# Row sums and exponential sums of an attention block moved between GpSimd, VectorE and TensorE

## The chip, the cores and the metric

The kernel runs on one core of a Trainium2 chip. A core has four engines that compute, each with an instruction queue of its own: TensorE (PE in the profile; PEld is its weight load), VectorE (DVE), ScalarE (ACT) and GpSimd (POOL). SyncE (SP) issues the DMAs. An engine takes its instructions in order; between engines the order is kept by semaphores. The metric is the device time of one execution in microseconds, median over runs.

## The reference

Two blocks follow each other. The first is attention with normalised queries and keys, for 8 batches of 12 heads, 448 positions, 64 elements a head:

```
q_n = q / sqrt(mean(q*q) + 1e-6) * g_q          # the same for k
scores = q_n @ k_n^T / 8
attn   = exp(scores - max); attn /= sum(attn)
x      = attn @ v                                # (8,12,448,64) -> (3584, 768)
```

The second takes the 3584 rows of x through `h = x @ w_in` (768 to 1024), `solu = h * softmax(h)`, a layer norm with gain, and `@ w_out` (1024 to 768). The change touches the first block only, in two places: the mean of squares under the square root, and the sum of the exponentials.

## The kernel before

Only `fast_path` runs on these inputs. Heads are taken four at a time: a quad m, of which there are 24 (0 to 23), is two pairs, a = 2m and b = 2m + 1, and a pair n is two heads. After the quads come the first product of the second block (line 989) and the last one (line 1203), each built of fewer, larger products of sums of blocks.

The order of all instructions is written out by hand, in the loop over m from line 1383 (`tc.manual_schedule()`), and each engine works in the order in which its instructions are emitted there. `unit(f)` emits a piece and then whatever was put off with `later`. The loop works on several quads at once. In the body of quad m:

- TensorE computes the scores of quad m, keys along partitions (`scores`, line 818): three tiles of 128 keys for each pair, `E0`, `E1`, `E2`, and one tile, `scores_last` (line 831), that holds the last 64 keys of both pairs. ScalarE takes the exponential of each as it comes (line 808; tiles of 128 x 896, two heads by 448 queries).
- Then `values_last` and `values` (lines 860 and 871) multiply the exponentials by v, and `sums` (line 890) adds the exponentials over the keys by products with a constant of ones, 32 columns wide, so that four of them fill the columns of the array. To spare TensorE some of these, VectorE has added `E0` and `E1` beforehand (`add`, line 845, tile `es`). In quads 0 to 21 `sums` runs over five tiles (the last keys, `E2` of each pair, `es` of each pair), each as four products; in the last two quads VectorE adds `E2` too (`add_more`, line 850) and `sums` runs over three.
- `inverse` transposes the sums and takes the reciprocal on VectorE (lines 901 and 902), and GpSimd copies parts of it across partitions (line 909, four small copies). In the next quad `divide` (lines 916 and 917) applies it and `store_x` writes x to memory.
- Beside it, quad m prepares what later quads need. `norms_next` completes 1/sqrt(mean of squares) for quad m + 1: two ScalarE instructions (lines 700 and 701) and four small ones on VectorE (lines 707 to 710, result `ny`), after which GpSimd scales q and k of the two pairs (`normalise`, line 719), VectorE transposes them (`qk_transpose`, line 729) and ScalarE applies the gains (line 733). For quad m + 2, ScalarE squares (line 662), VectorE sums 32 elements at a time (`row_sums`, line 670, tile `part`), and GpSimd joins the two halves of a head, which lie in neighbouring groups of 32 partitions: `fold_sums` copies the four groups across (line 680) and adds (line 681), which gives `ss`.
- Some quads convert a piece of w_in from 64-bit input: ScalarE (lines 535 and 536) in quads 4 to 10, 12, 14, 16, 18, 20, and VectorE's `join` (lines 541 and 542) one quad later each. `combine_in` (line 563, on GpSimd) forms differences of w_in blocks, in quads 9, 11, 13, 14, 15, 17, 19, 21 (one each) and 22, 23 (two each).

VectorE's order within quad m, from quad 5 on, is: reciprocal of quad m - 1 (901, 902), the four of `ny`, `divide` of quad m - 1, two transposes (729), `add(a)`, `row_sums` of pair a + 4, `row_sums` of pair b + 4, `add(b)`, and the join where there is one. GpSimd's is: copies of quad m - 1 (909), two `normalise`, `combine_in` where there is one, `fold_sums`.

PSUM tiles with tag "t" have three buffers of two banks each, shared by the score tiles and the sums tile; the pairs' outputs `o` have two buffers.

Of the kernel before, what the change touches and what calls it, by code (L numbers as in the profile page):

```python
# [9 lines left out]
FP32 = mybir.dt.float32  # L10
# [4 lines left out]
OP = AluOpType  # L15
# [351 lines left out]
def fast_path(  # L367
# [24 lines left out]
    nc = tc.nc  # L392
    B, H, S, D = q.shape
    DM, DFF = moe_w_in.shape
    P = 128
    NJ = S // P
    NB = S // 32
    NP = H // 2
    NQ = B * NP // 2
# [12 lines left out]
    consts = ctx.enter_context(tc.tile_pool(name="consts", bufs=1))  # L412
# [7 lines left out]
    work = first.enter_context(tc.tile_pool(name="work", bufs=2))  # L420
    ps_t = banks_in.enter_context(tc.tile_pool(name="ps_t", bufs=3, space=bass.MemoryType.PSUM))
    w_out = conv = sums_in = None

    ident = consts.tile([P, P], FP32, name="ident")
    ones = consts.tile([P, 3, 32], FP32, name="ones")

# [47 lines left out]
    def norm_gain():  # L474
        pg = ps_t.tile([P, KF], FP32, tag="t", name="pg")
        nc.tensor.transpose(pg, grow, ident[0:KF, 0:KF])
        nc.scalar.copy(gcol[:, 0:KF], pg)
# [81 lines left out]
    def combine(b, i):  # L559

        b11, b21, b22, t1, t3, t2, t4 = b
        o, p, q = [(t3, b22, t1), (t1, t1, b11), (t2, b22, t1), (t4, b21, t2)][i]
        nc.gpsimd.tensor_tensor(o, p, q, OP.subtract)  # L563

    def combine_in(x):
        c, i = divmod(x, 4)
        combine([w_in[k][:, c] for k in range(7)], i)
# [50 lines left out]
    st = {}  # L618
    quads = {}
    norms = {}  # L620
# [38 lines left out]
    def squares(n):  # L659
        d = st[n]  # L660
        d["sq"] = work.tile([P, 2 * NB, 32], FP32, tag="sq", name="sq", bufs=2)
        nc.scalar.activation(d["sq"].rearrange("p (s b) d -> p s (b d)", s=2), d["qk"], AF.Square)
# [3 lines left out]
    def row_sums(n):  # L666
        m, i = divmod(n, 2)
        if i == 0:
            norms[m] = {"part": small.tile([P, 2, 2 * NB], FP32, tag="part", name="part", bufs=2)}
        nc.vector.tensor_reduce(norms[m]["part"][:, i], st[n]["sq"], AX, OP.add)  # L670
# [3 lines left out]
    def fold_sums(m, e=nc.gpsimd):  # L674
        d = norms[m]
        part = d["part"].rearrange("p i b -> p (i b)")
        ss = d["ss"] = small.tile([P, 4 * NB], FP32, tag="ss", name="ss", bufs=2)
        for g in range(4):
            o = g ^ 1
            e.tensor_copy(ss[g * 32 : g * 32 + 32], part[o * 32 : o * 32 + 32])  # L680
        e.tensor_tensor(ss, ss, part, OP.add)
# [21 lines left out]
    def rsqrt_step(d):  # L703
# [5 lines left out]
        nc.vector.tensor_tensor(x, x, y, OP.mult)  # L709
        nc.vector.scalar_tensor_tensor(y, x, 1.5, y, OP.add, OP.mult)  # L710

    def normalise(n, e=nc.gpsimd):
        d = st[n]
        if ("one", n) in norms:
            y = norms["one", n]["y"]
        else:
            y = norms[n // 2]["y"][:, n % 2 * 2 * NB : (n % 2 + 1) * 2 * NB]
        d["qkn"] = work.tile([P, 2 * NB, 32], FP32, tag="qkn", name="qkn", bufs=2)
        e.tensor_tensor(  # L719
            d["qkn"].rearrange("p (s b) d -> p s b d", s=2),  # L720
            d["qk"].rearrange("p s (b d) -> p s b d", d=32),
            y.rearrange("p (s b) -> p s b ()", s=2).to_broadcast([P, 2, NB, 32]),
            OP.mult,
        )

    def qk_transpose(n):
        d = st[n]
        d["qkT"] = work.tile([P, 2, S], FP32, tag="qkT", name="qkT", bufs=3)
        nc.vector.transpose(d["qkT"].rearrange("p s t -> p (s t)"), d["qkn"].rearrange("p b d -> p (b d)"))  # L729
# [76 lines left out]
    def exponentials(d, kc, s):  # L806
        d["E", kc] = big_tile("E")[:, 0 : 2 * S].rearrange("p (h t) -> p h t", h=2)
        nc.scalar.activation(d["E", kc], s[:, :, 0:S], AF.Exp)  # L808

    def scores(n, kc):  # L810
        d = st[n]
        s = ps_t.tile([P, 2, 512], FP32, tag="t", name="s")

        for c in range(0, P, D):
            for h in range(2):
                hh = slice(h * D, (h + 1) * D)
                keys = slice(NJ * c + kc, NJ * (c + D - 1) + kc + 1, NJ)
                nc.tensor.matmul(  # L818
                    s[c : c + D, h, 0:S], d["qkT"][hh, 1, keys], d["qkT"][hh, 0, :],
                    start=True, stop=True,  # L820
                )
        exponentials(d, kc, s)
# [16 lines left out]
    def on_vector(m):  # L839
        return m >= NQ - 2  # L840

    def add(n):
        d = st[n]
        d["es"] = work.tile([P, 2, S], FP32, tag="es", name="es")
        nc.vector.tensor_tensor(d["es"], d["E", 0], d["E", 1], OP.add)  # L845

    def add_more(n):
        d = st[n]
        if on_vector(n // 2):
            nc.vector.tensor_tensor(d["es"], d["es"], d["E", 2], OP.add)  # L850
# [25 lines left out]
    def sums(m):  # L876


        d = quads[m]
        sm = d["sm"] = ps_t.tile([P, S // 2], FP32, tag="t", name="sm")  # L880
        terms = [(2, d["E", NJ])]
        for key in ("es",) if on_vector(m) else (2, "es"):
            for i in range(2):
                n = st[2 * m + i]
                terms.append((i, n["E", 2] if key == 2 else n["es"]))
        for x, (w, e) in enumerate(terms):
            for h in range(2):
                for t in range(2):
                    g = 32 * (2 * h + t)
                    nc.tensor.matmul(  # L890
                        sm[g : g + 32, :], ones[:, w], e[:, h, t * S // 2 : (t + 1) * S // 2],
                        start=(x == 0), stop=(x == len(terms) - 1),
                    )

    def inverse(m):


        d = quads[m]
        r = work.tile([P, NB // 2, 32], FP32, tag="r", name="r", bufs=1)
        rc = d["rc"] = small.tile([P, 2, 2, NB // 2], FP32, tag="rc", name="rc")  # L900
        nc.vector.transpose(r.rearrange("p b i -> p (b i)"), d["sm"])
        nc.vector.reciprocal(
            rc, r[:, :, 0:32:16].rearrange("p b i -> p i () b").to_broadcast([P, 2, 2, NB // 2])
        )
        for h in range(2):
            for t in range(2):
                a = 64 * h + 32 * t
                o = 64 * h + 32 * (1 - t)
                nc.gpsimd.tensor_copy(rc[o : o + 32, :, t], rc[a : a + 32, :, t])
# [405 lines left out]
    def unit(f, steps=4):  # L1315
        nonlocal now
        f()
        now += steps
        due = [x for x in todo if x[0] <= now]
        todo[:] = [x for x in todo if x[0] > now]  # L1320
        for _, g in sorted(due, key=lambda x: x[0]):
            g()
# [5 lines left out]
    joins_at = {9: (0,), 11: (1,), 13: (2,), 14: (3,), 15: (4,), 17: (5,), 19: (6,), 21: (7,), 22: (8, 9), 23: (10, 11)}  # L1328
# [34 lines left out]
    with tc.manual_schedule():  # L1363
# [19 lines left out]
        for m in range(NQ):  # L1383
            a, b = 2 * m, 2 * m + 1
# [9 lines left out]
            if m == 0:  # L1394
# [5 lines left out]
                for s in range(2):  # L1400
                    transpose_rows(1, s)
                    take_rows(1, s)
                squares(2)
                add(a)
                row_sums(2)
                fold_one(2)
# [10 lines left out]
                rsqrt_seed(norms["one", 3])  # L1417
                rsqrt_step(norms["one", 3])
                normalise(3)
                qk_transpose(2)  # L1420
                gain(2)
                add(b)
                unit(outputs)
                squares(4)
                qk_transpose(3)
                gain(3)
                unit(lambda: values(b))
                squares(5)
                unit(lambda: sums(m))
                inverse(m)  # L1430
                row_sums(4)
# [5 lines left out]
            def norms_next():  # L1437
                rsqrt_seed(norms[m + 1])
                rsqrt_step(norms[m + 1])
                normalise(a + 2)  # L1440
                normalise(b + 2)

            if early:
                norms_next()
            for x in joins_at.get(m, ()):
                combine_in(x)
            if next1:
                load_v(m + 1)
            if m == 1:
# [21 lines left out]
            unit(lambda: scores_last(m))  # L1471
            if m == 3:
                norm_gain()
            if m < 2:
                add(a)
            unit(lambda: scores(b, 0))
# [5 lines left out]
            unit(lambda: scores(b, 1))  # L1482
            if early or 1 < m < 4:
                qk_transpose(b + 2)
            if m > 1:
                add(a)
            unit(lambda: scores(b, 2))
            if m == 1:
                qk_transpose(a + 2)
            scarce = m < 5  # L1490
# [13 lines left out]
            if scarce and m > 1:  # L1504
                squares(b + 4)
                add(b)
            if next2:
                row_sums(b + 4)
                fold_sums(m + 2)
            if not scarce:  # L1510
                add(b)
            add_more(a)
            add_more(b)
            unit(outputs)
# [82 lines left out]
        for n in range(NS):  # L1597
            base = period * n
            for i, name in enumerate(ORDER):
# [4 lines left out]
                x = HALVES[name][0]  # L1604
# [118 lines left out]
```

## Time and profile before

| | us |
|---|---|
| median of 3 runs (lowest, highest) | 816.29 (816.02, 816.68) |
| the profiled execution | 815.47 |
| its span, first to last instruction | 813.7 |
| TensorE busy in the span | 797.9 |
| VectorE, ScalarE, GpSimd busy | 617.0, 473.9, 469.0 |
| one quad, from quad 5 to 21 | 12.90 |

The sums below are made against the profiled execution: span 813.7 us and 1.8 us outside it, 815.47 us, which is 0.8 us under the median. The attention block ends 325.5 us after the start, the first product of the second block at about 560 us. TensorE's rows count two instructions for each fp32 product. Starts and durations are in us unless marked ns; the text after an arrow in brackets names what ended the idle time before an instruction.

### The profile page before, as it was taken

The page shows a single profiled execution, that of the slowest core. Times are in us where ns is not written, and L with a number is a line of the kernel's source. Part 1 is how long each engine was busy: PE and PEld are TensorE (multiplying, and loading weights), DVE is VectorE, ACT ScalarE, POOL GpSimd, SP SyncE. Part 2 cuts the span into 40 slices and gives each one's busy share as a digit, 9 for nine tenths or more (in the row PEclk, how much of TensorE's full clock was granted, in tenths as well). Part 3 has the DMA queues.
Part 4 walks back from the last instruction along what each step waited for, and adds up shares of the span by engine and source line. Part 5 has one row for each costly group of instructions (what it writes and reads, how often), then busy time and mean ns, then how long its engine had stood idle before and what let it go on. Part 6 is the DMA issues. An engine that isn't in the chain of part 4 may idle for free.

```text
span 813.7 us, 14586 instructions
## 1 busy us (share of the span) xinstructions
PE 797.9 (98%) x5030; PEld 468.4 (58%) x5030; DVE 617.0 (76%) x1217; ACT 473.9 (58%) x785; POOL 469.0 (58%) x635
## 2 busy tenths in 40 slices
PE   8999999999999999999999999999989999999997
PEld 4334444444444443444444444444679999999996
DVE  6877889888887977478878756777796876866945
ACT  6677878777786865365767545444515454464420
POOL 1353555656555566233356467767497867777761
PEclk9999999999999999999999999999999999999999
DMA  9868798887878644245755344552548457365412
GB/s 165 175 143 157 165 184 185 188 178 159 163 162 180 132 94 123 81 131 142 184 142 146 91 113 122 147 137 64 171 122 279 129 197 245 122 239 181 150 60 83
DMA packets 269600, 122.71 MB, mean 151 GB/s; under 512 B 187596, under 2 KB 254668, under 8 KB 269516
## 3 DMA queue, kind: packets, MB, share of 16 engines
q1 hardware_dynamic: 254332, 111.78, 55.1%
q10 hardware_dynamic: 15184, 9.90, 4.5%
q8 instruction: 42, 0.69, 0.4%
q14 instruction: 42, 0.34, 0.1%
HBM read 84.94 MB, written 36.70 MB: 149 GB/s over the span
## 4 chain that ended last, share of the span: by engine, by line
PE 88%; DVE 5%; POOL 2%; DMA 2%; ACT 2%; issue 1%; SPq 0%; DVEq 0%; POOLq 0%; ACTq 0%
PE A L1203 14%; PE A L989 13%; PE o L871 13%; PE s L818 12%; PE B L989 8%; PE B L1203 7%; PE sm L890 5%; PE C L989 4%; PE D L989 4%; PE C L1203 3%; PE o L860 2%; PE s L831 2%; DMA xg<-xd 1%; ACT E L808 1%; DVE bs L1072 1%
## 5 line engine op out<-in xcount | busy, mean ns | idle before, releaser
L808 ACT ACTIVATE E<-s 128x896 f32<-128x896 f32 x168 | 139.1, 937 | 20.3 <-PE s L818 20.0
L818 PE MATMUL s<-qkT 64*64 64x448 f32 x1152 | 120.5, 545 | 1.4 <-ACT E L808 0.7
L871 PE MATMUL o<-E,v 128*64 128x448 f32 x576 | 113.5, 543 | 0.0
L680 POOL COPY ss<-part 32x56 f32<-32x56 f32 x88 | 42.1, 478 | 91.5 <-DVE part L670 88.8
L719 POOL TENSOR_TENSOR qkn<-qk,ny 128x896 f32<-128x896 f32 x46 | 77.1, 1697 | 21.2 <-DMA qk<-in_k_dram 12.0
L1078 POOL TENSOR_TENSOR he<-he,mhalf 128x1 f32<-128x1 f32 x28 | 27.6, 986 | 105.6 <-DVE he L1077 105.1
L1203 PE MATMUL B<-w_out,sums 128*128 128x192 f32 x392 | 80.0, 327 | 3.3 <-DVE P L1265 2.1
L818 PEld LDWEIGHTS s<-qkT 64*64 64x64 f32 x1152 | 48.1, 163 | 59.6 <-ACT E L808 29.2
L1203 PE MATMUL A<-w_out,sums 128*128 128x192 f32 x392 | 80.0, 327 | 1.2 <-POOL sums L1183 0.8
L871 PEld LDWEIGHTS o<-E,v 128*64 128x64 f32 x576 | 39.2, 137 | 72.7 <-issue 67.3
L989 PE MATMUL B<-w_in,xsum 128*128 128x512 f32 x168 | 76.7, 592 | 0.7 <-POOL he L1078 0.7
L989 PE MATMUL A<-w_in,xg 128*128 128x512 f32 x168 | 74.6, 593 | 0.0
L1060 ACT ACTIVATE u<-h,hmax 128x1024 f32<-128x1024 f32 x28 | 32.2, 1148 | 63.4 <-DVE hmax L1054 63.3
L1203 PEld LDWEIGHTS B<-w_out,sums 128*128 128x128 f32 x392 | 66.1, 190 | 4.0 <-DVE P L1265 2.4
L1203 PEld LDWEIGHTS A<-w_out,sums 128*128 128x128 f32 x392 | 66.1, 190 | 2.1 <-POOL sums L1183 1.3
L989 PEld LDWEIGHTS B<-w_in,xsum 128*128 128x128 f32 x168 | 31.8, 190 | 41.2 <-issue 38.3
L989 PEld LDWEIGHTS A<-w_in,xg 128*128 128x128 f32 x168 | 31.8, 190 | 40.1 <-issue 39.6
L845 DVE TENSOR_TENSOR es<-E 128x896 f32<-128x896 f32 x48 | 53.4, 1114 | 1.3 <-ACT E L808 1.3
L670 DVE TENSOR_REDUCE part<-sq 128x28 f32<-128x896 f32 x46 | 48.1, 1078 | 2.4
L729 DVE STREAM_TRANSPOSE qkT<-qkn 128x896 f32<-128x896 f32 x46 | 48.5, 1088 | 1.8 <-POOL qkn L719 1.8
L1203 PE MATMUL A<-w_out,s 128*128 128x192 f32 x224 | 45.5, 326 | 0.0
L563 POOL TENSOR_TENSOR w_out<-w_out 128x384 f32<-128x384 f32 x44 | 44.5, 1017 | 1.3
(151 smaller groups left out, 1622.4 us busy)
## 6 DMA issues: line engine op xcount, KB each, us to landing
ur<-ud SPq DMA_DIRECT2D x60, 256.0 KB, 4.5
ud<-ub SPq DMA_DIRECT2D x112, 128.0 KB, 2.3
xd<-xo SPq DMA_DIRECT2D x48, 224.0 KB, 3.1
qk<-in_q_dram SPq DMA_DIRECT2D x92, 112.0 KB, 3.1
qk<-in_k_dram SPq DMA_DIRECT2D x92, 112.0 KB, 3.0
v<-in_v_dram SPq DMA_DIRECT2D x24, 384.0 KB, 4.4
out_dram<-P SPq DMA_DIRECT2D x19, 384.0 KB, 3.7
raw<-in_moe_w_in_dram SPq DMA_DIRECT2D x12, 512.0 KB, 4.7
```

The lines of the kernel that those rows point to most:

```text
L563: nc.gpsimd.tensor_tensor(o, p, q, OP.subtract)
L670: nc.vector.tensor_reduce(norms[m]["part"][:, i], st[n]["sq"], AX, OP.add)
L680: e.tensor_copy(ss[g * 32 : g * 32 + 32], part[o * 32 : o * 32 + 32])
L719: e.tensor_tensor(d["qkn"].rearrange("p (s b) d -> p s b d", s=2), d["qk"].rearrange("p s (b d) -> p s b d", d=32), y.rearrange("p (s b) - ...
L729: nc.vector.transpose(d["qkT"].rearrange("p s t -> p (s t)"), d["qkn"].rearrange("p b d -> p (b d)"))
L808: nc.scalar.activation(d["E", kc], s[:, :, 0:S], AF.Exp)
L818: nc.tensor.matmul(s[c : c + D, h, 0:S], d["qkT"][hh, 1, keys], d["qkT"][hh, 0, :], start=True, stop=True,)
L845: nc.vector.tensor_tensor(d["es"], d["E", 0], d["E", 1], OP.add)
L871: nc.tensor.matmul(d["o"][h * D : (h + 1) * D, :], quads[n // 2]["v"][:, n % 2 + 2 * h, kc], d["E", kc][:, h], start=False, stop=(kc == NJ ...
L890: nc.tensor.matmul(sm[g : g + 32, :], ones[:, w], e[:, h, t * S // 2 : (t + 1) * S // 2], start=(x == 0), stop=(x == len(terms) - 1),)
L989: nc.tensor.matmul(k[bank], a[:, c], w_in[i][:, c], start=begin and c == 0, stop=c == HD - 1, skip_group_check=not begin,)
L1203: nc.tensor.matmul(k[bank], a[:, c].rearrange("p a i -> p (a i)"), w_out[:, area, i, c], start=begin and c == 0, stop=c == KC - 1, skip_gr ...
```

## The change

In quads 5 to 21 (`settled`):

1. `add_late` puts `E1 + E2` of each pair on GpSimd, and VectorE's `add` then adds `E0` to that. `sums` therefore runs over three tiles instead of five in all quads from 5 on.
2. `fold_sums` is gone. In its place TensorE multiplies `part` by a 128 x 128 constant, `halves`, at the end of `sums`. The result `ss` lies in the second bank of the PSUM buffer whose first bank holds the sums, so this buffer is held until line 707 has read `ss` in the next quad.
3. VectorE's `add(b)` comes before `row_sums` of pair b + 4 and no longer after it; `combine_in` moves on GpSimd from before the scores to after both new additions.

`fill_halves` makes the constant once, on GpSimd, in quad 4.

```
+    def settled(m):
+        return 4 < m < NQ - 2
+    def add_late(n):
+        d = st[n]
+        d["es"] = work.tile([P, 2, S], FP32, tag="es", name="es")
+        nc.gpsimd.tensor_tensor(d["es"], d["E", 1], d["E", 2], OP.add)
     def add(n):
         d = st[n]
+        if settled(n // 2):
+            nc.vector.tensor_tensor(d["es"], d["E", 0], d["es"], OP.add)
+            return
...
-        sm = d["sm"] = ps_t.tile([P, S // 2], FP32, tag="t", name="sm")
+        two = ps_t.tile([P, 2, 512], FP32, tag="t", name="sm")
+        sm = d["sm"] = two[:, 0, 0 : S // 2]
         terms = [(2, d["E", NJ])]
-        for key in ("es",) if on_vector(m) else (2, "es"):
+        for key in ("es",) if m > 4 else (2, "es"):
...
+        if settled(m):
+            d = norms[m + 2]
+            d["ss"] = two[:, 1, 0 : 4 * NB]
+            nc.tensor.matmul(
+                d["ss"], halves, d["part"].rearrange("p i b -> p (i b)"), start=True, stop=True
+            )
...
-            for x in joins_at.get(m, ()):
-                combine_in(x)
+            if not settled(m):
+                for x in joins_at.get(m, ()):
+                    combine_in(x)
...
             unit(lambda: scores(b, 1))
             if early or 1 < m < 4:
                 qk_transpose(b + 2)
+            if settled(m):
+                add_late(a)
             if m > 1:
                 add(a)
             unit(lambda: scores(b, 2))
+            if settled(m):
+                add_late(b)
...
+            if settled(m):
+                add(b)
             if next2:
                 row_sums(b + 4)
-                fold_sums(m + 2)
-            if not scarce:
+                if not settled(m):
+                    fold_sums(m + 2)
+            if m >= NQ - 2:
                 add(b)
+            if settled(m):
+                for x in joins_at.get(m, ()):
+                    combine_in(x)
```

More of the change, by code (lines that the diff above doesn't have):

```diff
@@ L422, in fast_path @@
     w_out = conv = sums_in = None
+    halves = consts.tile([P, P], FP32, name="halves")
     ident = consts.tile([P, P], FP32, name="ident")
@@ L710, in rsqrt_step, with fill_halves @@
         nc.vector.scalar_tensor_tensor(y, x, 1.5, y, OP.add, OP.mult)
+    def fill_halves():
+        x = ident.rearrange("p (h x t) -> p h x t", h=2, x=2)
+        nc.gpsimd.tensor_tensor(
+            halves.rearrange("p (h x t) -> p h x t", h=2, x=2),
+            x[:, :, 0:1].to_broadcast([P, 2, 2, 32]), x[:, :, 1:2].to_broadcast([P, 2, 2, 32]), OP.add,
+        )
     def normalise(n, e=nc.gpsimd):
@@ L893, in sums @@
                     )
+        if settled(m):
[3 more added lines that the diff above has]
+                d["ss"], halves, d["part"].rearrange("p i b -> p (i b)"), start=True, stop=True
+            )
     def inverse(m):
@@ L1473, in fast_path @@
                 norm_gain()
+            if m == 4:
+                fill_halves()
             if m < 2:
```

## The prediction

> **What bounds the kernel now.** I read the engines' totals and the chain that ended last, then the chain in order of time within one quad, then each engine's timeline over the same quad. From the page:
>
> ```profile
> PE 797.9 (98%) x5030; PEld 468.4 (58%) x5030; DVE 617.0 (76%) x1217; ACT 473.9 (58%) x785; POOL 469.0 (58%) x635
> ...
> PE 88%; DVE 5%; POOL 2%; DMA 2%; ACT 2%; issue 1%; SPq 0%; DVEq 0%; POOLq 0%; ACTq 0%
> ```
>
> TensorE is the bound. The chain in order of time (start, duration) shows quad 14, from 197.16:
>
> ```profile
> 197.16 2.45 PE s L818 x24
> 199.61 0.75 PE s L831 x8
> 200.36 2.25 PE s L818 x24
> 202.61 0.75 PE o L860 x8
> 203.37 4.66 PE o L871 x24
> 208.03 2.03 PE sm L890 x40
> ```
>
> These touch one another and add up to 12.9: a quad is 12.90 because TensorE's work is 12.90, and its last 2.03 are the 40 instructions of the sums. The other engines have to come round once in that time; how nearly they fail to is in the timelines of VectorE and GpSimd:
>
> ```profile
> 194.91 0.72 DVE L541 SCALAR_TENSOR_TENSOR tmp<-raw,tmp 128x512 uint32<-128x512 uint32 x1
> 195.66 0.69 DVE L542 SCALAR_TENSOR_TENSOR w_in<-raw,tmp 128x512 uint32<-128x512 uint32 x1
> 197.22 0.42 DVE L901 STREAM_TRANSPOSE r<-sm 128x224 f32<-128x224 f32 x1 [0.87 <-PE sm L890]
> ...
> 198.68 0.22 DVE L710 SCALAR_TENSOR_TENSOR ny<-nx,ny 128x56 f32<-128x56 f32 x1
> ...
> 203.63 1.05 DVE L845 TENSOR_TENSOR es<-E 128x896 f32<-128x896 f32 x1
> 204.81 2.08 DVE L670 TENSOR_REDUCE part<-sq 128x28 f32<-128x896 f32 x2
> 206.80 1.08 DVE L845 TENSOR_TENSOR es<-E 128x896 f32<-128x896 f32 x1
> ```
>
> ```profile
> 199.10 3.36 POOL L719 TENSOR_TENSOR qkn<-qk,ny 128x896 f32<-128x896 f32 x2
> 202.41 1.28 POOL L563 TENSOR_TENSOR w_in<-w_in,w_in 128x512 f32<-128x512 f32 x1
> 207.02 1.75 POOL L680 COPY ss<-part 32x56 f32<-32x56 f32 x4 [3.33 <-DVE part L670]
> 208.85 0.30 POOL L681 TENSOR_TENSOR ss<-ss,part 128x56 f32<-128x56 f32 x1
> ```
>
> VectorE finishes the join of a quad only 0.87 before it has to read the sums. GpSimd has holes, but its two normalise end at 202.46, 5.3 into the quad, and all that is queued behind them starts after that.
>
> **The change part by part.**
>
> *TensorE, less.* Two of five tiles leave the sums: 16 of 40 instructions at 2.03 / 40 = 0.051, so 0.81 a quad. Quad 22 already has that shape.
>
> *TensorE, more.* The product with `halves` is two instructions, 128 x 128 weights and 112 columns. Nearest rows: 8 transposes of 112 x 112 at the start take 1.22, 0.15 each, and 392 instructions of 128 x 192 on line 1203 take 80.0, 0.20 each. So 0.3 to 0.4; I take 0.3. TensorE alone would need 12.90 - 0.81 + 0.30 = 12.39 a quad, 17 x 0.51 = 8.7 us less in all. That is what the change can give.
>
> *GpSimd, less.* Copies and add, 1.75 + 0.30 up to 2.58 + 0.30. They were behind the loop that follows, so removing them yields nothing on the path.
>
> *GpSimd, more.* Two additions of 128 x 896 with two full operands. Undisturbed additions of that kind took 0.725 for 256 columns (minimum 0.724, line 1181), 1.00 for 384 (median of line 563 on w_out) and 1.28 for 512 (median on w_in): 0.00216 us a column and 0.17 fixed, so 2.10 for 896. The lowest bound is `normalise`, also 128 x 896 but with one operand repeated along 32 elements: 1.70. I take 2.10, since shape and operands are those of the three rows; 1.70 and 2.20 stay as ends.
>
> By the Trainium skill's page "GPSIMD Engine Reference", section "Elementwise — side-by-side cycle accounting", a tensor_tensor add of 2048 columns takes 4497 ns, scaled an estimate of 1.97 for ours, and its section "Engine selection" advises VectorE for such an add; at 1.97 the sum below would be 34 x 0.13 = 4.4 lower. No run here shows that row, and the 2.10 of the rows is kept.
>
> *Who has the port.* VectorE's `add` and GpSimd's additions exclude each other, as two places show. At 207.02 the first copy of line 680 meets `add(b)`, started at 206.80, and the four take 1.75 instead of 1.02 as at 79.05. And where VectorE asks just after GpSimd:
>
> ```profile
> 599.79 0.73 POOL L1182 TENSOR_TENSOR sums<-sums,s 128x256 f32<-128x256 f32 x1
> ```
>
> ```profile
> 599.84 1.23 DVE L1164 TENSOR_TENSOR s<-ur 128x512 f32<-128x512 f32 x1
> ```
>
> GpSimd has its undisturbed 0.73, and VectorE, 0.05 later, 1.23 instead of 0.72. Now `add(a)` waits for `add_late(a)`. Released by GpSimd, VectorE starts 0.03 after its end (199.05 after 199.01, lines 916 and 909), while GpSimd's next instruction starts 0.04 before the end of the last, if its inputs are there (two normalise: 3.36 for 2 x 1.70). E2 of pair b is there: ScalarE's seven exponentials end 6.8 into the quad. So `add_late(b)` gets the port first and `add(a)` waits for both, 4.20 after the second normalise. Had VectorE got it, its 1.05 would lie between the two additions, and `add(b)` would come 1.05 sooner. That is the other end.
>
> *VectorE.* Behind the waiting `add(a)` are queued the two row sums, `add(b)`, the join, and line 901 of this quad, which all move back. `add(b)` before the second row sum: 1.05 sooner for TensorE's sums, 1.05 later for `part`, for which the `halves` product now waits, and behind it all scores of the next quad and their exponentials.
>
> *The loop.* From one `ny` (end of line 710) to the next, all in sequence:
>
> - normalise both pairs: 202.46 - 198.90 = 3.56
> - two additions on GpSimd: 4.20
> - add, row sum, add, row sum on VectorE: 1.05 + 1.04 + 1.05 + 1.04 = 4.18
> - with a join: 1.44 for it (194.91 to 196.35), then lines 901 to 710: 198.90 - 197.22 = 1.68. Sum 15.06, with hand-offs 15.1.
> - without a join: the product 0.3 and its hand-off 0.1, lines 700 and 701 0.62 (197.13 to 197.75), lines 708 to 710 0.75, hand-offs 0.1: 1.87. Sum 13.8.
>
> Before, no such loop existed: the adds needed nothing from GpSimd, and the fold came after them with room. Now it outlasts TensorE's 12.39 in every quad, so TensorE waits, for `es` of pair b, then for `part`. Twelve quads have a join (5 to 11, 13, 15, 17, 19, 21), five have none: 12 x 15.1 + 5 x 13.8 = 250.2, against 17 x 12.90 = 219.3: +30.9.
>
> *combine_in, moved.* It has no reader before line 989, so the move itself costs nothing. But it now follows the additions: `add(a)`, which already waits, goes first, then 1.28 of combine_in runs beside 1.04 of row sum and holds `add(b)` for 0.24: eight quads, +1.9. Between nothing and 1.28 each.
>
> *PSUM buffer.* It is wanted by the third score tile, 1.65 into the quad; line 707 reads `ss` at 0.8 now, and some 1.8 in a quad after a join. TensorE has slack there by then. Nothing; 0.2 a quad at most.
>
> *DMA queue and the rest.* No DMA is moved in SP's order; store_x and the loads wait for divide and stretch with the quads. `fill_halves`, one 128 x 128 addition in a GpSimd hole of quad 4: under 0.5, hidden by the 4.6 it idles there. After quad 21 the lateness of `ny` reaches the end by divide, the store and the reload of x for the second block, which in the chain already sets the start of quad 23. Everything later is shifted.
>
> Sum: 30.9 + 1.9 = +32.8 on 815.47: 848.3; on the median, 0.8 more, **849 us**.
>
> **The rivals.**
>
> 1. *VectorE takes the port between the two additions.* Then 17 x 1.05 = 17.9 less, so 831. For it: at 594 to 600 a VectorE instruction that is already waiting gets in between two of GpSimd. Against it: here it isn't yet waiting. 0.13.
> 2. *A cheaper addition.* At 1.70 the loops are 14.3 and 13.0: 34 x 0.40 = 13.6 less, 835. For it: line 719, the same size. Against: the three rows with two full operands. 0.13.
> 3. *Faster: the loop closes in time, and TensorE's saving is all that is left.* One mechanism, the price of GpSimd's addition. With p for it, 12 x (10.9 + 2p) + 5 x (9.6 + 2p) = 219.3 at p = 1.19: below that there is no loss, and at 0.75 the joined loop fits 12.39 and 808 is reached. For it: GpSimd idles 44% of these quads (busy 122.6 of 219.3), and TensorE is 98% busy. Against: no 128 x 896 row of GpSimd is under 1.69. 0.07.
> 4. *More than I count*: combine_in holding `add(b)` fully, or TensorE's pauses dearer: 8 x 1.04 more, 858 and beyond. 0.07.
>
> **How the numbers follow.** My case 0.58, rivals 0.13, 0.13, 0.07, 0.07, and 0.02 for no change. The time is that of my case. Its own range is 841 to 853 (2.0 to 2.2 an addition, combine_in 0 to 0.5). The range of 8 in 10 takes in rivals 1 and 2 with their mid-values and leaves out 3 and most of 4: 826 to 857. A change under 0.2% (1.6 us) can't be told from none. Faster 0.08, same 0.02, slower 0.90.
>
> **What would show it.** Right: GpSimd's additions at 2.1 each, back to back; `add(a)` recorded with some 3 us where its own time is 1.05; quads of 15 and 13.8 us, alternating from 12 on; TensorE idle before `sm`, put down to `es`, and before the scores or the product, put down to `part`; DVE and POOL with large shares of the chain between 81 and 300 us. Wrong: quads of 12.4, no wait of TensorE for line 845; additions under 1.7; or `add(a)` at 1.05 between two additions of GpSimd (rival 1). What happens after 325 us should only be shifted.

## The result

The changed kernel takes 842.79 us (median; 842.55 to 844.07) against 816.15 for the kernel before in the same comparison: a ratio of 1.0331, 95% interval 1.0313 to 1.0349. It is 26.6 us slower. The forecast was 849, with a range from 826 to 857.

The profiled execution's span went from 813.7 to 841.0 us, 27.3 more. TensorE's starts of the first scores of each quad divide it: quads 5 to 21 take 244.9 instead of 219.3 (+25.6), quads 22 and 23 take 25.9 instead of 25.2 (+0.7), and all that follows 489.2 instead of 488.2 (+1.0). So the loss lies in the quads that were changed.

From the page of the changed kernel: the busy times, the chain's shares by engine, and three of the costly groups (busy time, mean ns of one, then idle time ahead of them and what ended it). Line numbers have moved, and differ a little from run to run: 856 is GpSimd's new addition, 861 VectorE's add behind it, 917 the product with `halves`, 927 the transposition of the sums (901 before), 701 the first ScalarE instruction of `ny`, 671 the row sums.

```profile
PE 803.5 (96%) x4792; PEld 462.2 (55%) x4792; DVE 649.1 (77%) x1217; ACT 472.1 (56%) x785; POOL 506.1 (60%) x585
...
PE 62%; DVE 21%; POOL 11%; ACT 2%; DMA 2%; issue 1%; SPq 0%; DVEq 0%; POOLq 0%; ACTq 0%
...
L861 DVE TENSOR_TENSOR es<-E,es 128x896 f32<-128x896 f32 x34 | 67.8, 1993 | 15.3 <-POOL es L856 15.3
...
L856 POOL TENSOR_TENSOR es<-E 128x896 f32<-128x896 f32 x34 | 71.5, 2126 | 0.4 <-ACT E L816 0.4
...
L701 ACT ACTIVATE ny<-sm,eps 128x56 f32<-128x56 f32 x17 | 5.2, 308 | 76.2 <-DVE r L927 76.2
```

From the page of the kernel before, VectorE's add:

```profile
L845 DVE TENSOR_TENSOR es<-E 128x896 f32<-128x896 f32 x48 | 53.4, 1114 | 1.3 <-ACT E L808 1.3
```

TensorE carried 88% of the chain and now carries 62%. VectorE and GpSimd carry 32%, where it was 7%. VectorE's add has a mean of 1993 ns where the same shape took 1114; the mean is of two kinds, as the rows below show, about 2.98 us for `add(a)` and 1.1 for `add(b)`. One turn of the loop, quad 13, is in the chain in order of time (start, duration):

```profile
199.32 3.35 POOL qkn L727 x2
202.67 2.08 POOL es L856
204.75 0.02 issue
204.77 2.98 DVE es L861
207.75 1.00 DVE part L671
208.74 1.09 DVE es L861
209.83 1.00 DVE part L671
210.83 0.61 DVE tmp L542
211.44 0.02 issue
211.46 0.69 DVE w_in L543
212.15 0.34 DVE r L927
212.49 0.02 issue
212.51 0.33 DVE rc L928
212.84 0.01 issue
212.85 0.23 DVE nx L708
...
214.03 3.35 POOL qkn L727 x2
```

TensorE does not appear at all. From `normalise` to the next `normalise` everything is GpSimd's and VectorE's, 14.71 long. (In a quad without a join, TensorE's product is in it, with 0.44.) What TensorE does in the meantime is in its timeline (line 910 is the sums):

```profile
208.11 0.58 PE L910 MATMUL sm<-E,ones 128*32 128x224 f32 x8
208.51 0.56 PE L910 MATMUL sm<-es,ones 128*32 128x224 f32 x8
209.88 0.58 PE L910 MATMUL sm<-es,ones 128*32 128x224 f32 x8 [0.81 <-DVE es L861]
210.88 0.43 PE L917 MATMUL sm<-part,halves 128*128 128x56 f32 x2 [0.41 <-DVE part L671]
```

It waits for `es` of the second pair, then for `part`, the two waits that were forecast.

### The profile page after: what moved, and what is told of

The parts are those of the page before. It is cut to its first block, busy times and chain, and to the rows that moved or that the text cites. A ratio compares the mean times of both kernels' runs of the same rounds, so it can differ in the third digit from the quotient of the medians.

```text
span 841.0 us, 14056 instructions
## 1 busy us (share of the span) xinstructions
PE 803.5 (96%) x4792; PEld 462.2 (55%) x4792; DVE 649.1 (77%) x1217; ACT 472.1 (56%) x785; POOL 506.1 (60%) x585
## 4 chain that ended last, share of the span: by engine, by line
PE 62%; DVE 21%; POOL 11%; ACT 2%; DMA 2%; issue 1%; SPq 0%; DVEq 0%; POOLq 0%; ACTq 0%
PE A L1229 14%; PE A L1015 12%; PE B L1015 8%; DVE es L861 8%; PE B L1229 7%; POOL qkn L727 6%; PE C L1015 4%; DVE part L671 4%; PE D L1015 4%; POOL es L856 4%; PE C L1229 3%; PE o L890 3%; PE s L826 3%; PE sm L910 1%; DVE w_in L543 1%
## 5 line engine op out<-in xcount | busy, mean ns | idle before, releaser
L826 PE MATMUL s<-qkT 64*64 64x448 f32 x1152 | 127.2, 561 | 3.6 <-DVE nx L708 2.1
L826 PEld LDWEIGHTS s<-qkT 64*64 64x64 f32 x1152 | 45.8, 165 | 65.1 <-ACT E L816 33.4
L935 POOL COPY rc<-rc 32x14 f32<-32x14 f32 x96 | 19.8, 206 | 100.1 <-DVE rc L928 86.5
L861 DVE TENSOR_TENSOR es<-E,es 128x896 f32<-128x896 f32 x34 | 67.8, 1993 | 15.3 <-POOL es L856 15.3
L856 POOL TENSOR_TENSOR es<-E 128x896 f32<-128x896 f32 x34 | 71.5, 2126 | 0.4 <-ACT E L816 0.4
L701 ACT ACTIVATE ny<-sm,eps 128x56 f32<-128x56 f32 x17 | 5.2, 308 | 76.2 <-DVE r L927 76.2
```

Of the source, the lines that this page charges most:

```text
L826: nc.tensor.matmul(s[c : c + D, h, 0:S], d["qkT"][hh, 1, keys], d["qkT"][hh, 0, :], start=True, stop=True,)
L856: nc.gpsimd.tensor_tensor(d["es"], d["E", 1], d["E", 2], OP.add)
L861: nc.vector.tensor_tensor(d["es"], d["E", 0], d["es"], OP.add)
```

## The experiments

The theory: the loss is a loop, from `ny` over two normalise and two additions on GpSimd to VectorE's adds, row sums and join, and back to `ny`. It is longer than TensorE's work of a quad. Its rivals: the product with the constant, with `ss` in PSUM, is what costs; or VectorE and GpSimd are too full for any addition on GpSimd; or it does not matter who gets the port they share (by the rows in the prediction, a two-input add of VectorE and an addition of GpSimd exclude each other; "the port" stands for what they exclude each other from). Lengths of a quad below are from TensorE's first score to the next quad's first score, read from each run's timeline.

### The product alone

VectorE and TensorE add as before the change, and VectorE's order is the old one; the product is kept, and with it the new place of `combine_in`. Part of the edit:

```
...
-        for key in ("es",) if m > 4 else (2, "es"):
+        for key in ("es",) if on_vector(m) else (2, "es"):
...
-            if settled(m):
-                add_late(a)
...
-            if settled(m):
-                add_late(b)
...
-            if settled(m):
-                add(b)
...
```

> Only the product with the constant replaces GpSimd's copies in quads 5 to 21; the exponentials are added as before the change (VectorE E0 + E1, TensorE takes E2), and add(b) is again behind the row sums. Loop theory (the loss is the chain from ny over both normalise and both GpSimd additions to VectorE's adds and back to ny): without the additions the chain is short, TensorE is the bound again and pays only for the product, 0.36 a quad in the changed kernel's trace, 17 x 0.36 = 6.1: 822, quads of 13.26, no wait of TensorE for part. Rival, the product theory (the loss is ss in PSUM: TensorE waits for part and line 701 for line 927): quads of 14 and more, above 835.

Measured: 822.65 us (822.27 to 824.43), ratio 1.0087 (1.0071 to 1.0104). Every quad from 5 to 21 takes 13.25 or 13.26. The chain of this run:

```profile
211.13 2.03 PE sm L907 x40
213.16 0.36 PE sm L914 x2
213.52 2.45 PE s L826 x24
```

TensorE goes from the sums to the product to the scores with no pause. The product costs its own 0.36 and nothing else, and the new place of `combine_in` costs nothing by itself. As the cause of the loss the product falls.

### The additions alone

GpSimd keeps the fold of four copies and an add; no product:

```
-        if settled(m):
-            d = norms[m + 2]
-            d["ss"] = two[:, 1, 0 : 4 * NB]
-            nc.tensor.matmul(
-                d["ss"], halves, d["part"].rearrange("p i b -> p (i b)"), start=True, stop=True
-            )
...
-                if not settled(m):
-                    fold_sums(m + 2)
+                fold_sums(m + 2)
```

> Only GpSimd's additions; the fold stays with GpSimd, behind them, as four copies and an add. Loop theory: the loop now has the fold in it. From the changed kernel's rows 3.49 + 5.08 + 1.00 + 1.09 + 1.00 = 11.66 up to the second row sum, then 1.4 fold (2.3 beside a join), 0.66 and 0.75 to ny: 14.5 and 15.4 a quad, and combine_in before the next normalise some 0.9 in eight quads: 854 to 861, say 858, slower than the changed kernel. Product theory: the waits for part go and TensorE saves 0.81 a quad: 802 to 805.

Measured: 858.10 us (857.56 to 859.03), ratio 1.0519 (1.0501 to 1.0537). Quads behind one with a join take 15.3, without one 14.5, and 16.0 behind one with both a join and a combine_in (15.5 behind quad 14, which has a combine_in and no join). TensorE has less work here than in the changed kernel, and the time is the longest of all. In this order of instructions the product thus earned its 0.36: it took GpSimd's fold out of the loop. The two halves of the change do not add up (+6.5 and +42.0 alone, +26.6 together): with the additions in place, the product removes a piece of the loop.

### VectorE's row sums before both adds

```
-            if m > 1:
+            if m > 1 and not settled(m):
                 add(a)
...
-            if settled(m):
-                add(b)
             if next2:
                 row_sums(b + 4)
...
+            if settled(m):
+                add(a)
+                add(b)
```

> As the changed kernel, but VectorE takes both row sums before both adds, so that they fill the time in which it waited for GpSimd. Loop theory: the loop loses both row sums: 3.49 + 5.08 + 1.00 + join 1.30 + 1.75 = 12.6 with a join, and without one TensorE's own 12.45. In the eight quads with a combine_in, that one holds the port between the two adds, 1.2 each. Sum over 17 quads 223.5 against 219.3: 820; 811 if VectorE's second add goes ahead of combine_in. Rival, full engines (the additions and the shared port cost this much in whatever order): 835 to 843, quads of 14 and more.

Measured: 822.65 us (822.09 to 823.16), ratio 1.0079 (1.0063 to 1.0096), 20 us less than the changed kernel by order alone. Row sums wait for nothing of GpSimd and have one input, so they run while GpSimd adds: two of them take 2.08 from 180.85 on, beside two additions of GpSimd that take 4.18 from 178.56 on. Quads without a combine_in take 12.87, those with one 13.65 to 13.95. That GpSimd and VectorE are too full in whatever order is excluded. The second effect, combine_in, shows in the timeline of VectorE, once without and once with:

```profile
182.84 2.08 DVE L861 TENSOR_TENSOR es<-E,es 128x896 f32<-128x896 f32 x2
...
195.57 3.01 DVE L861 TENSOR_TENSOR es<-E,es 128x896 f32<-128x896 f32 x2
```

Two adds take 2.08 alone, and 3.01 when a combine_in takes the port between them (GpSimd's row: 1.28 from 195.35 on). What the new place of `add(b)` in the changed kernel does by itself was not tried.

### Who gets the port, with a wait

A copy of a column of `es` stands between GpSimd's two additions and makes the second wait for VectorE's `add(a)`:

```
             if settled(m):
+                turn = small.tile([P, 1], FP32, tag="turn", name="turn", bufs=2)
+                nc.gpsimd.tensor_copy(turn, st[a]["es"][:, 0, 0:1])
                 add_late(b)
```

> As the changed kernel, but a copy of one column of es of pair a stands between GpSimd's two additions, so that the second can only start when VectorE's add(a) is done: VectorE gets the port in between. Loop theory: add(a) takes 1.0 instead of 2.98, the second addition ends about 1.25 later, add(b) starts 0.5 to 0.6 sooner than in the changed kernel: 17 x 0.55 = 9.4 less, 833. If who goes first did not matter: 843 or some us above, for the copy.

Measured: 842.37 us (841.91 to 843.23), ratio 1.0321 (1.0303 to 1.0338): no gain over the changed kernel, and a miss of 9. By the number alone the port would not matter. The timeline of VectorE says otherwise:

```profile
203.51 1.09 DVE L861 TENSOR_TENSOR es<-E,es 128x896 f32<-128x896 f32 x1 [0.84 <-POOL es L856]
204.52 1.08 DVE L671 TENSOR_REDUCE part<-sq 128x28 f32<-128x896 f32 x1
206.93 2.14 DVE L861 TENSOR_TENSOR es<-E,es 128x896 f32<-128x896 f32 x1 [1.33 <-POOL es L856]
```

`add(a)` fell from 2.98 to 1.09, as expected. But `add(b)`, which now waits for the second addition directly, meets the same race again: combine_in is next in GpSimd's queue, and `add(b)` takes 2.14. Quads without a combine_in (5 to 8 and 10) average 14.07 instead of 14.47; the odd ones from 9 on, which have one, 14.70 instead of 14.25. I had priced the first race and overlooked the second.

### Who gets the port, without a wait

```
             if settled(m):
+                gap = small.tile([P, 1], FP32, tag="turn", name="turn", bufs=2)
+                nc.gpsimd.tensor_copy(gap, mhalf)
                 add_late(b)
...
             if settled(m):
+                gap = small.tile([P, 1], FP32, tag="turn", name="turn", bufs=2)
+                nc.gpsimd.tensor_copy(gap, mhalf)
                 for x in joins_at.get(m, ()):
                     combine_in(x)
```

> As the changed kernel, but on GpSimd a copy of one column of a constant, which waits for nothing, stands behind each of the two additions. It takes 0.18 and only moves GpSimd's next request for the port from 0.04 before the end of the addition to about 0.1 after it; VectorE's request comes 0.03 after it. If who asks first decides, VectorE now goes first both times: add(a) about 1.1 instead of 2.98, the second addition recorded with some 3, add(b) 3.15 after the start of add(a) instead of 3.89, and in front of combine_in instead of behind it. 0.75 to 0.87 a quad, 17 times: 12.8 to 14.8 less than the changed kernel, 829 (827 to 832). If the order of requests does not decide, 843 or some us more, and add(a) stays near 3.

Measured: 828.59 us (828.30 to 832.21), ratio 1.0170 (1.0145 to 1.0196), 14.2 below the changed kernel. A short copy on GpSimd behind each addition, whose result nobody reads, changes who waits. Quads 5 to 21 take 13.6 of the 14.2. GpSimd's timeline and VectorE's:

```profile
196.26 2.11 POOL L856 TENSOR_TENSOR es<-E 128x896 f32<-128x896 f32 x1
198.31 0.19 POOL L1521 COPY turn<-mhalf 128x1 f32<-128x1 f32 x1
198.45 3.00 POOL L856 TENSOR_TENSOR es<-E 128x896 f32<-128x896 f32 x1
```

```profile
198.41 1.09 DVE L861 TENSOR_TENSOR es<-E,es 128x896 f32<-128x896 f32 x1 [0.84 <-POOL es L856]
199.41 1.08 DVE L671 TENSOR_REDUCE part<-sq 128x28 f32<-128x896 f32 x1
201.49 1.09 DVE L861 TENSOR_TENSOR es<-E,es 128x896 f32<-128x896 f32 x1 [0.99 <-POOL es L856]
```

VectorE starts at 198.41 and takes 1.09; GpSimd starts 0.04 later and takes 3.00, which is its 2.1 and VectorE's rest. In the changed kernel it was the other way round, 2.98 for VectorE and 2.1 for GpSimd. The changed kernel holds the same trial by chance. In quad 12 the second addition had to wait 0.37 for `E2`, behind a stretch in which TensorE was slow (last section), and VectorE's `add(a)` came first:

```profile
191.29 1.09 DVE L861 TENSOR_TENSOR es<-E,es 128x896 f32<-128x896 f32 x1 [0.84 <-POOL es L856]
```

```profile
191.62 2.73 POOL L856 TENSOR_TENSOR es<-E 128x896 f32<-128x896 f32 x1 [0.37 <-ACT E L816]
```

The order of the two starts decides. In the attention block of all ten profiles there are 88 pairs of a VectorE add of exponentials and an addition or combine_in of GpSimd with starts under 0.2 apart, 76 of them under 0.1. In every one the instruction that started first kept its own time and the other got longer. The Trainium skill's page "SBUF — State Buffer", section "Who interferes with whom", says that a VectorE instruction with two SBUF inputs contends with a GpSimd instruction that reads SBUF, and that issue order decides which of the two blocks. The 2.98 and 3.00 of the two runs agree with it.

### One pair only, the first

GpSimd adds `E1 + E2` for the first pair only and folds again; combine_in is right behind the addition and VectorE's order is that of the kernel before. The first part of the edit:

```
-        if settled(n // 2):
+        if settled(n // 2) and n % 2 == 0:
...
+                if key == 2 and settled(m) and i == 0:
+                    continue
...
```

> The mirror of the run with the second pair: GpSimd adds E1 + E2 of the first pair only, combine_in right behind it, the fold is GpSimd's, VectorE's order is that of the kernel before. Loop theory: add(a) waits for GpSimd (some 0.9) with the row sums, add(b) and the join behind it: 3.5 + 2.1 + 1.0 + 2.0 + 1.05 + 1.35 + 1.75 = 12.7 in a quad with a join, 12.49 (TensorE) without: 12 x 12.7 + 5 x 12.49 = 214.9 against 219.3, 4 less, 812 (808 to 816), behind the run with the second pair. Full engines: 816 or more, and the two pairs alike.

Measured: 824.84 us (824.58 to 825.29), ratio 1.0113 (1.0098 to 1.0129), 13 above what I expected. By the number alone the rival, full engines, fits (816 or more); but it also has the two pairs alike, and the second pair, below, takes 808.77. Behind the first, quads take 13.06 to 13.47, but 14.2 in quads 9 and 14 and 13.9 in 11. VectorE's join is not the leg that closes this loop: the fold is. GpSimd's timeline:

```profile
99.35 2.10 POOL L856 TENSOR_TENSOR es<-E 128x896 f32<-128x896 f32 x1
104.69 2.58 POOL L681 COPY ss<-part 32x56 f32<-32x56 f32 x4 [3.25 <-DVE part L671]
107.36 0.30 POOL L682 TENSOR_TENSOR ss<-ss,part 128x56 f32<-128x56 f32 x1
```

The addition delays `add(a)`, that delays the row sums, and these the fold, whose copies then meet `add(b)` and the join at the port (2.58; 1.02 where nothing meets them). Normalise to normalise is 109.21 - 96.04 = 13.17. And combine_in right behind the addition wins the same race against `add(a)` (2.16 in quad 9), which I had not carried over.

### Both pairs, row sums first, GpSimd's fold

The edits of the run with the row sums first, and the fold on GpSimd in place of the product.

> Both pairs on GpSimd, VectorE's row sums before both adds, and GpSimd folds instead of the product; combine_in behind the fold. TensorE alone would need 12.09 a quad, 802 in all. Loop theory: normalise 3.5, additions 4.15, fold beside add, add and join 2.8 to 4.1 (its copies and VectorE's two-input instructions take turns at the port), 1.4 to ny: 11.9 without a join, 13.2 with one, and combine_in delays the next normalise by some 0.9 in eight quads: 12 x 13.2 + 5 x 12.1 + 7 = 226: 823 (816 to 830). If the product were what costs: 802 to 806.

Measured: 819.89 us (818.78 to 820.58), ratio 1.0051 (1.0035 to 1.0066). Quads take 12.4 to 13.6, within the forecast. TensorE's lowest need, 12.09, is reached in none. Against the additions alone, with the same instructions, VectorE's order saves 38 us (858.10 to 819.89). And with the row sums first the fold is 2.8 cheaper than the product (822.65): what the product earned above hangs on the order.

### One pair only, the second

```
+        if settled(n // 2) and n % 2 == 1:
+            nc.vector.tensor_tensor(d["es"], d["E", 0], d["es"], OP.add)
+            return
...
+                if key == 2 and settled(m) and i == 1:
+                    continue
...
             unit(lambda: scores(b, 2))
+            if settled(m):
+                add_late(b)
```

With `settled` and `add_late` as in the change, these are all its edits to the kernel before.

> From the kernel before: in quads 5 to 21 GpSimd adds E1 + E2 of the second pair only, VectorE adds E0 to it; the first pair, the order of VectorE, GpSimd's fold and the place of combine_in stay. Loop theory: this leaves no loop. E2 of pair b is there 6.85 into the quad, GpSimd's normalise end at 5.35, so combine_in (1.28) fits in front; add(a) needs nothing of GpSimd and fills 6.6 to 7.65, the addition runs 7.65 to 9.75 beside the two row sums, which use one input, and add(b) follows them at 9.75 as before. TensorE stays the bound and loses one of five tiles, 0.41 a quad: 17 x 0.41 = 7.0 less, 809 (806 to 813), quads of 12.49. Rival, full engines (any addition of 2.1 on GpSimd costs, since VectorE and GpSimd have no room): 816 or more.

Measured: 808.77 us (808.07 to 810.29), ratio 0.9918 (0.9904 to 0.9932): 0.8% faster than the kernel before. All 17 quads take 12.52. Its chain in order of time is TensorE's alone again, with 32 instructions of sums instead of 40:

```profile
193.80 2.45 PE s L818 x24
196.25 0.75 PE s L831 x8
197.00 2.26 PE s L818 x24
199.25 0.75 PE o L871 x8
200.00 4.66 PE o L882 x24
204.66 1.65 PE sm L903 x32
```

An addition on GpSimd is free here, because VectorE comes to the add that needs it only after it has ended (190.93 after 190.78 in one quad, though it is recorded with 2.63). `add(a)` needs nothing of GpSimd and starts before GpSimd's addition wants the port, the two row sums run beside that addition, and combine_in lies where GpSimd has to wait for the scores of the second pair anyway.

Quad lengths side by side; the groups are quads 5 to 8 and 10, the odd ones from 9 to 21, quad 14, and 12, 16, 18, 20:

```
                         5-8,10   9..21 odd   14      12,16,18,20   median us
before                   12.90    12.90       12.90   12.90         816.15
changed                  14.47    14.25       14.72   14.52         842.79
product alone            13.26    13.26       13.26   13.26         822.65
additions alone          14.98    14.87       16.01   16.01         858.10
row sums first           12.85    13.74       13.89   12.87         822.65
port, with a wait        14.07    14.70       15.47   14.18         842.37
port, without a wait     13.69    13.31       13.92   13.92         828.59
first pair only          13.08    13.46       14.23   13.47         824.84
rows first, fold back    13.06    12.69       13.55   13.55         819.89
second pair only         12.52    12.52       12.52   12.52         808.77
```

## Why the prediction was right, point by point

The mechanism, the sign and the places of the waits were as forecast. The size was 6 too high. The prediction's own range for its case, 841 to 853, does not follow from its bounds: 2.0 to 2.2 an addition and 0 to 0.5 for each combine_in give 844 to 855, and the measured 842.8 lies just below that. The wide range held it.

- *The addition on GpSimd.* Forecast 2.10 from the three rows with two full operands; measured 2.09 at the least and 2.11 in the median of 34. The 1.70 of `normalise` was the wrong neighbour. The estimate of 1.97 from the Trainium skill's page "GPSIMD Engine Reference", section "Elementwise — side-by-side cycle accounting", is 0.14 under the measured 2.11; the extrapolated rows were nearer.
- *Who gets the port.* Forecast from a start 0.03 after against one 0.04 before; `add(a)` took 2.97 to 2.99 in 16 of the 17 quads, and 1.09 in quad 12, where VectorE came first. Rival 1 was priced at 17.9; the run without a wait measures it, two races together, at 14.2.
- *The loop with a join.* Forecast 15.1, measured 14.62 to 14.73 in eleven of twelve intervals from `ny` to `ny` (14.96 in the other). The mis-sized terms are the two additions with the add (forecast 5.25, in the chain 2.08 + 0.02 + 2.98 = 5.08) and the join (1.44, in the chain 1.32). I had added durations of instructions that follow each other on one engine; there a next one starts before the last has ended, as in the row 207.67 with 1.07 followed by 208.66.
- *The loop without a join.* Forecast 13.8, measured 13.90 to 14.01 from quads 14, 16, 18 and 20, and 13.48 from quad 12, the one in which VectorE got the port. That 13.8 came out so near is partly luck, since two errors cancel: the pieces ahead of the product were too large, as above, and the term of 1.87 behind the second row sum was too small by 0.5. I had line 701 and, on VectorE, line 708 go on right behind the product. But line 927 waits for the product too, and both stand behind it (quad 14):

```profile
225.60 0.44 PE sm L917 x2
226.04 0.02 issue
226.07 0.43 DVE r L927
```

```profile
226.52 0.31 ACT L701 ACTIVATE ny<-sm,eps 128x56 f32<-128x56 f32 x1 [3.65 <-DVE r L927]
```

Line 701 starts 0.02 to 0.03 after the end of line 927 in each of the 17 quads. The two ways from there are equally long: lines 928 and 708 on VectorE end at 227.09, lines 701 and 702 on ScalarE at 227.11. So it is the 0.43 of line 927 that was left out, and not the wait of line 701 alone.

- *The product.* Forecast 0.3, measured 0.36. Its columns are 56 and not 112 as I wrote; `part` holds 56 numbers a partition. The price hardly moved with that; what sets it was not tried. The sums of three tiles take 1.27 and save 0.76, not 0.81, so TensorE alone would need 12.50 and not 12.39, which is not on the path. The removal of GpSimd's fold was put at nothing; with the additions in front of it, it is worth 15.3 (858.10 against 842.79).
- *combine_in.* Forecast +1.9 over eight quads by 0.24 each. In the loop shown, `add(b)` is 1.17 long where it is 1.08 undisturbed, and the loop with a join is 14.71 to 14.73 with a combine_in and 14.62 or 14.63 without (quads 6, 7, 8 and 10): about 0.1, since the row sum beside it hides nearly all. That is 1.2 too much.
- *The PSUM buffer.* Put at nothing, 0.2 a quad at most. In eleven of the twelve quads behind one with a join, TensorE waits 0.15 to 0.21 there, for line 708; the chain does not pass there.
- *The sum.* 12 x 15.1 + 5 x 13.8 + 1.9 = 252.1 was forecast; the 17 intervals from `ny` of quad 5 to that of quad 22 are 245.7 (328.53 - 82.83). The end of the chain, with divide and the reload of x, passed it on. So the loop was forecast 6.4 too long, nearly all of it in the quads with a join; the 1.0 that the rest of the kernel lost, where only a shift was forecast, hides a part of that, which is luck.
- *Rival 3*, faster, is excluded by the same rows: no addition under 2.09, where 1.19 was needed. What it had right shows in the run with the second pair: TensorE's saving, 0.38 a quad there, is real once the loop is gone.

## What to carry to other kernels

Before work is given to an engine that is 56% busy, draw the loop that its result closes, with everything queued behind the instruction that waits for it: here sparing TensorE 0.76 us a quad cost some 1.5, and half of the offer, placed where nobody waited, gained 0.4. Where VectorE and GpSimd both read two tiles from SBUF, the first to start held the other up until it was done (2.98 for 1.09, 3.00 for 2.1), so what stands next in GpSimd's queue counts as much as what is added. In this kernel VectorE's row sums, with one input, belong beside GpSimd's additions, and its two-input adds behind them.

## What was not expected

In the changed kernel TensorE's clock falls to half for 3.4 us, twice before its last microseconds; two windows, the columns ahead of the last two being the granted clock:

```profile
183.40:186.80 3.40, 3.40 (x24) 1.33 (x20) 3.06 (x9) 2.06 (x4) 1.81 (x5) 0.50 0.65 198
620.30:623.70 3.40, 3.40 (x13) 3.40 (x12) 1.34 (x5) 0.00 (x0) 3.32 (x5) 0.50 0.87 223
```

The first comes after pauses of 1.14 and 0.41 in quad 11, the second after one of 2.15 on line 1229. All ten kernels have a pause of 2.1 at that place of the last product; six, the changed one among them, have a half-clock window right behind it, and four, the kernel before among them, kept the full clock. From the end of the last sums on, the six take 488.9 to 489.2 and the four 488.1 to 488.7. So the 1.0 us that the rest of the kernel lost goes with the window; that the window is all of it was not tried. The Trainium skill's page "TensorE: Matmul & The Clock Gate", section "Why this matters for your kernels", asks for no idle gap over some 3 us; here shorter ones were enough in two places and not in many others, so what decides stays open.

That line 701 waits for line 927, though they read different banks of the PSUM buffer, is shown by the starts; why the wait is there, and why line 927, which reads the sums alone, waits for the product, was not tried.
